# Respacing the first and the last transform of an interleaved SSM and FFN kernel

## The chip, the cores and the metric

The kernel runs on one core of one Trainium2 chip. The metric is the device time of one execution in microseconds (us), the median of three runs. Engines are called by their names or by those of the profile: TensorE (PE; PEld is its weight load), VectorE (DVE), ScalarE (ACT), GpSimd (POOL), and SyncE (SP), whose queue starts most DMA transfers.

## The reference

The reference computes the output and all gradients of a block that adds two branches to its input: an S4 layer (a long convolution whose filter comes from complex exponentials) and a gated feed-forward network with a ReLU gate. Cut to what matters:

```python
# x, grad_out: [1, 2048, 576] bf16; W_gate, W_up: [576, 4608]; W_down: [4608, 576]; A, B, C: [576, 128]
xn = layernorm(x)
# branch A: S4
dt = exp(log_dt)
P  = exp(dt * (A_re + 1j * A_im) [:, :, None] * arange(2048))
K  = einsum("dn,dnl,dn->dl", C, P, dt * B).real
y  = irfft(rfft(xn padded) * rfft(K padded))[:2048] + xn * Dskip
# branch B: gated feed-forward
gate = xn @ W_gate; gate = gate * (gate > 0)
h    = gate * (xn @ W_up)
out  = x + y + h @ W_down
# returned: out, and the gradients of x, A, B, C, log_dt, Dskip, W_gate, W_up, W_down for grad_out
```

## The kernel before

There are two sources of work. The feed-forward part (FFN) runs through 12 slices of the hidden dimension, c = 0 to 11, and is TensorE work nearly throughout. The S4 part is a Python generator that puts its instructions between those of the FFN. Each source yields its estimated us, and the driver lets the S4 part have the fraction `PACE` of the FFN's:

```python
PACE = 0.9
for us in ffn.gen(ln, final):
    if us == "last":                  # the final output needs the S4 part
        if s4_open: ...               # emit what is left of it
        continue
    ft += us
    ...
    while s4_open and stt < PACE * (ft - start):
        r = next(sgen, None)
        if r is None: s4_open = False
        else: stt += r
```

So a larger number yielded by the S4 part spreads the same instructions over more FFN work. A scheduler then sets the order in each engine's queue, near to this one.

The convolution is done by DFT in three stages per half of the 576 channels. `p1` transforms the input and the output gradient and brings the filter's gradient back; `p2` makes the filter and the parameter gradients; `p3` transforms the filter and brings back the results. Between the stages the data go through DRAM, because the next stage needs them in another layout. A pause (`yield gap`) gives the stores and the first loads time. `n` is the number of buffers: 4 where a transform stands alone in the kernel (the first, `p1(0)`, and the last, `p3(1)`), 2 or so where it runs beside `p2`.

```python
def both(self, a, wa, b, wb):         # interleaves two tasks in the ratio wa : wb
    ta = tb = 0.0
    for us in a:
        ta += us
        yield us
        while b is not None and tb * wa < ta * wb: ...   # next step of b, yielded too

def slow(self, f, task):
    for us in task: yield f * us

# in gen():
yield from self.both(self.p1(0, 4, 10.0), 68.0, self.params(pw), 45.0)
with ExitStack() as c:
    pools = self.p2_pools(c)
    yield from self.both(self.p2(0, pools, pw), 0.8 * W2, self.p1(1, 2, 3.0), W1)
    yield from self.both(self.p2(1, pools, pw), 0.8 * W2, self.p3(0, 2, 3.0), W3)
yield from self.p3(1, 4, 8.0)
```

The forward stage, line 628 in the profile, for ns signals (2 in `p1`, 1 in `p3`):

```python
def fwd1(self, hf, ns, load, ap, op, n, gap):
    ...
    for n2 in range(ST):              # ST = 16
        if n2 % 2 == 0:
            S1, sig = Sx.get(n2 // 2), sigs.get(n2 // 2)
            if n2 == 0: yield gap
        A = op.tile([P, 2, ns, DH], BF16, name=f"fA{ns}")          # DH = 288
        for ri in range(2):
            for i in range(ns):
                ps = self.ps()        # one of 3 PSUM buffers of the S4 part
                nc.tensor.matmul(ps[:, :DH], lhsT=S1[:, n2 % 2, ri, :], rhs=sig(i, n2), start=True, stop=True)
                g.bal.copy(A[:, ri, i, :], ps[:, :DH], DH)         # on VectorE or ScalarE
            if ri == 0: yield 0.2 * ns
        nc.sync.dma_start(self.A[ns][hf][:, n2], A[:])
        yield 0.2 * ns
```

The mixing stage (line 645, and 655 on the way back) and the back stage (line 686) of `p1`:

```python
    f = 1.0 if n < 4 else 1.25
    for h in range(ST + 1):
        if h < ST:
            b = bs.get(h)             # load of b_ug, n ahead
            if h == 0: yield gap
            for i in range(2):
                yield from self.slow(f, self.mix(sg[:, i], b[:, :, i, :]))
                yield f * 0.15
            ...                       # store of s_ug
            Z = self.product(fp, pp, sg[:, 1], sg[:, 0], True)
            yield f * 0.7
        if old is not None:
            yield from self.slow(f, self.unmix(Ct[:, :, 0, :], old))
            ...                       # store of C_dk
            yield f * 0.5
    # back stage: loads of bC1 in n + 1 buffers
    for n2 in range(ST):
        Ct = cs.get(n2)
        if n2 == 0: yield gap
        ...
        g.bal.copy(dk[:, :, n2 % 4, :], self.back2(S3[:, n2 % 2], Ct, 0)..., DH)
        yield 0.5
```

`p3` has a forward stage and a mixing stage (f = 2.0) alike. Its results (`C_ydu`, loaded as `bC2`) go into the output matmuls of the last FFN slice.

Beside `p1(0)` runs `params`. It loads the S4 parameters, makes their products, and in 36 steps the decay exponentials, each a multiplication on VectorE, an exponential on ScalarE and a store of 320 KB:

```python
def ex_step(i):
    v.tensor_tensor(ex[:], pw[:, 0, ...], self.ev[...], op=ALU.mult)      # line 585
    nc.scalar.activation(ex[:], ex[:], ACT.Exp)                            # line 586
    nc.sync.dma_start(self.ex_dram[:, i], ex[:])
    bal.add(d=0.75, a=0.65)
for i in range(0, 8):
    ex_step(i)
    yield 1.0
...                                   # products of the parameters, yields of 2 x 2.0
for i in range(8, D // SX):           # 8 to 35
    ex_step(i)
    yield 1.0
```

Of the kernel before, what the change touches and what calls it, by code (L numbers as in the profile page):

```python
# [20 lines left out]
L, D, F, N = 2048, 576, 4608, 128  # L21
# [10 lines left out]
SX = 16  # L32
# [61 lines left out]
def iota(nc, ap, pattern, base, mult):  # L94
    nc.gpsimd.iota(ap, pattern=pattern, base=base, channel_multiplier=mult, allow_small_or_imprecise_dtypes=True)
# [380 lines left out]
class S4:  # L476
# [85 lines left out]
    def params(self, pw):  # L562

        g, nc, bal = self.g, self.g.nc, self.g.bal
        v = nc.vector
        with ExitStack() as c:
            pool = self.pool(c, "par_raw", 1)
            exp_ = self.pool(c, "par_ex", 8)
            raw = pool.tile([P, 6, D], BF16, name="raw")
            nc.sync.dma_start(raw[:], self.par_in[:])  # L570
            ldt = pool.tile([P, D], BF16, name="ldt")
            nc.sync.dma_start(ldt[:], self.log_dt.rearrange("(o d) -> o d", o=1).to_broadcast([P, D]))
            yield 1.0
            dt = pool.tile([P, D], F32, name="dtf")
            nc.scalar.activation(dt[:], ldt[:], ACT.Exp)
            nc.sync.dma_start(self.dt_dram[:], dt[:])
            Ar, Ai, Br, Bi, Cr, Ci = (raw[:, i, :] for i in range(6))
            v.tensor_tensor(pw[:, 0, :], Ar, dt[:], op=ALU.mult)
            bal.add(d=0.7, a=0.7)
            yield 1.0  # L580

            def ex_step(i):
                shp = [P, SX, NE]
                ex = exp_.tile(shp, F32, name="exs")
                v.tensor_tensor(ex[:], pw[:, 0, i * SX:(i + 1) * SX].unsqueeze(2).to_broadcast(shp), self.ev[:].unsqueeze(1).to_broadcast(shp), op=ALU.mult)
                nc.scalar.activation(ex[:], ex[:], ACT.Exp)
                nc.sync.dma_start(self.ex_dram[:, i], ex[:])
                bal.add(d=0.75, a=0.65)

            for i in range(0, 8):  # L590
                ex_step(i)
                yield 1.0
            p1 = pool.tile([P, D], F32, name="p1")
            p2 = pool.tile([P, D], F32, name="p2")
            v.scalar_tensor_tensor(pw[:, 1, :], Ai, 1.0 / TWO_PI, dt[:], op0=ALU.mult, op1=ALU.mult)
            for j, (y1, y2, op) in enumerate(((Br, Bi, ALU.subtract), (Bi, Br, ALU.add))):
                v.tensor_tensor(p1[:], Cr, y1, op=ALU.mult)
                v.tensor_tensor(p2[:], Ci, y2, op=ALU.mult)
                v.tensor_tensor(p1[:], p1[:], p2[:], op=op)
                v.tensor_tensor(pw[:, 2 + j, :], p1[:], dt[:], op=ALU.mult)  # L600
                bal.add(d=2.6)
                yield 2.0
            for i in range(8, D // SX):
                ex_step(i)
                yield 1.0

# [82 lines left out]
    def p1(self, hf, n, gap):  # L689

        g, nc = self.g, self.g.nc
        cols = slice(hf * DH, (hf + 1) * DH)
        with ExitStack() as c:
            ap = self.pool(c, f"p1_a{hf}", n, "right")

            def load(m):
                t = ap.tile([P, 2, 2, DH], BF16, name="sig")
                nc.sync.dma_start(t[:, 0], g.xn_dram[:, 2 * m:2 * m + 2, cols])
                nc.sync.dma_start(t[:, 1], g.g_v[:, 2 * m:2 * m + 2, cols])
                return lambda i, n2: t[:, i, n2 % 2, :]  # L700
            yield from self.fwd1(hf, 2, load, ap, self.pool(c, f"p1_o{hf}", 2 * n - 2 * (n < 4), "right"), n, gap)
        with ExitStack() as c:
            bp = self.pool(c, f"p1_b{hf}", n, "right")
            fp = self.pool(c, f"p1_f{hf}", n, "right")
            pp = self.pool(c, f"p1_p{hf}", 1, "right")

            def load_b(h):
                b = bp.tile([P, 2, 2, DH], BF16, name="b_ug")
                nc.sync.dma_start(b[:], self.mix_in(self.A[2][hf], h))
                return b  # L710
            bs = Ahead(load_b, ST, n)
            Z = None
            f = 1.0 if n < 4 else 1.25
            for h in range(ST + 1):
                old, Z = Z, None
                if h < ST:
                    b = bs.get(h)
                    if h == 0:
                        yield gap
                    sg = fp.tile([P, 2, 2, DH], BF16, name="s_ug")  # L720
# [3 lines that stand above are left out]
                    nc.sync.dma_start(self.S[hf][h], sg[:])  # L724
# [3 lines that stand above are left out]
                    Ct = fp.tile([P, 2, 1, DH], BF16, name="fC1")  # L728
                    yield from self.slow(f, self.unmix(Ct[:, :, 0, :], old))
                    nc.sync.dma_start(self.mix_in(self.C[1][hf], h - 1), Ct[:])  # L730
                    yield f * 0.5
        with ExitStack() as c:
            bp = self.pool(c, f"p1_c{hf}", n + 1, "right")
            dp = self.pool(c, f"p1_d{hf}", 2, "right")

            def load_c(n2):
                Ct = bp.tile([P, 2, 1, DH], BF16, name="bC1")
                nc.sync.dma_start(Ct[:], self.C[1][hf][:, n2])
                return Ct
            Sx, cs = Ahead(self.dft(bp, self.s3_dram), ST // 2, n), Ahead(load_c, ST, n + 1)  # L740
            for n2 in range(ST):
                if n2 % 2 == 0:
                    S3 = Sx.get(n2 // 2)
                Ct = cs.get(n2)
                if n2 == 0:
                    yield gap
                if n2 % 4 == 0:
                    dk = dp.tile([P, DH // SC, 4, SC], BF16, name="dk")
                g.bal.copy(dk[:, :, n2 % 4, :], self.back2(S3[:, n2 % 2], Ct, 0).rearrange("p (g d) -> p g d", d=SC), DH)
                if n2 % 4 == 3:  # L750
                    nc.sync.dma_start(self.dk_dram[hf][:, n2 // 4], dk[:])
                yield 0.5

    def p3(self, hf, n, gap):

        g, nc, bal = self.g, self.g.nc, self.g.bal
        with ExitStack() as c:
            ap = self.pool(c, f"p3_a{hf}", n, "right")
            kp = self.pool(c, f"p3_k{hf}", 2, "right")
            kks = [None]  # L760

            def load(m):
                if m % 2 == 0:
                    kks[0] = kp.tile([P, DH // SC, 4, SC], BF16, name="kk")
                    nc.sync.dma_start(kks[0][:], self.k_dram[hf][:, m // 2])
                kk = kks[0]
                return lambda i, n2: kk[:, :, n2 % 4, :]
            yield from self.fwd1(hf, 1, load, ap, self.pool(c, f"p3_o{hf}", 2 * n - 2 * (n < 4), "right"), n, gap)
        with ExitStack() as c:
            bp = self.pool(c, f"p3_b{hf}", n, "right")  # L770
            fp = self.pool(c, f"p3_f{hf}", n, "right")
# [11 lines left out]
            f = 1.0 if n < 4 else 2.0  # L783
# [234 lines left out]
    def gen(self):  # L1018
        g, nc = self.g, self.g.nc
        self.make_dft16()  # L1020
        yield 1.0
        yield from self.make_dft128()
        with ExitStack() as cp:
            kp = self.pool(cp, "s4_par", 1)
            pw = kp.tile([P, 4, D], F32, name="pw")
            self.ev = kp.tile([P, NE], F32, name="ev")
            self.ones = kp.tile([P, 1], F32, name="ones")
            nc.vector.memset(self.ones[:], 1.0)
            iota(nc, self.ev[:, 0:16], [[1, 16]], 0, 0)
            iota(nc, self.ev[:, 16:24], [[256, 8]], 0, 0)  # L1030
            iota(nc, self.ev[:, 24:40], [[16, 16]], 0, 0)
            yield from self.both(self.p1(0, 4, 10.0), 68.0, self.params(pw), 45.0)
            with ExitStack() as c:
                pools = self.p2_pools(c)
                yield from self.both(self.p2(0, pools, pw), 0.8 * W2, self.p1(1, 2, 3.0), W1)
                yield from self.both(self.p2(1, pools, pw), 0.8 * W2, self.p3(0, 2, 3.0), W3)
            yield from self.p3(1, 4, 8.0)

class Final:

# [214 lines left out]
```

## Time and profile before

| | before |
|---|---|
| median of 3 runs | 1794.33 us |
| lowest, highest | 1794.07, 1795.59 us |
| span of the profiled execution | 1792.3 us |
| instructions in it | 42070 |
| DMA moved | 373.30 MB, mean 208 GB/s |
| share of packets' time on SyncE's queue (q1) | 52.4% of 16 engines |

The first transform runs from 95 to 285 us of the span, the parameter stage with the second and third transform beside it from about 300 to 1480 us, and the last transform from 1493 to 1619 us. A stretch of the span is read by the busy us of each engine in it, against its length.

### The profile page before, as it was taken

What the parts mean: (1) busy time and instruction counts of PE and PEld (TensorE: products, weight loads), DVE (VectorE), ACT (ScalarE), POOL (GpSimd) and SP (SyncE); (2) the same over time, 40 slices, a digit from 0 to 9 for tenths busy, and PEclk for the clock granted to TensorE, in tenths of its full rate; (3) what the DMA queues carried; (4) which work ended last, traced back from release to release, by engine and by line L of the source; (5) the groups of instructions that cost most, each with busy time, mean ns of one, the idle gap of its engine ahead of it and who ended that gap; (6) DMA issues with size and microseconds to landing.
All of it is one profiled execution on the core that took longest, in us unless ns stands there. A gap on an engine that the chain in (4) does not pass through costs nothing.

```text
span 1792.3 us, 42070 instructions
## 1 busy us (share of the span) xinstructions
PE 1719.7 (96%) x16449; PEld 1184.7 (66%) x16449; DVE 1317.8 (74%) x2867; ACT 1189.2 (66%) x2736; POOL 205.0 (11%) x246
## 2 busy tenths in 40 slices
PE   7989989999999999999999999999999998999998
PEld 5665557667667666766766766766676675676776
DVE  7575884677789788678787889889978962972551
ACT  5875874786688477568468658747857845864651
POOL 0200112011022011012101101101111100110000
PEclk9999999999999999999999999999999999999999
DMA  9799989679568656766858856866766578995873
GB/s 297 265 332 303 331 233 295 194 182 253 165 145 228 192 139 157 226 183 147 229 154 190 230 156 142 212 188 151 181 185 152 112 212 257 260 288 157 270 240 100
DMA packets 239004, 373.30 MB, mean 208 GB/s; under 512 B 49491, under 2 KB 153429, under 8 KB 237269
## 3 DMA queue, kind: packets, MB, share of 16 engines
q1 hardware_dynamic: 212836, 304.09, 52.4%
q0 software_dynamic: 24384, 51.92, 18.6%
q10 hardware_dynamic: 1584, 14.60, 2.3%
q8 instruction: 129, 2.11, 0.5%
q14 instruction: 71, 0.57, 0.1%
HBM read 233.10 MB, written 137.43 MB: 207 GB/s over the span
## 4 chain that ended last, share of the span: by engine, by line
PE 63%; DVE 21%; ACT 7%; DMA 6%; issue 3%; SPq 1%; POOL 0%; ACTq 0%; DVEq 0%; POOLq 0%
PE ps_mm L298 17%; PE ps_mm L244 15%; PE ps_mm L352 11%; PE ps_mm L336 6%; PE ps_mm L270 3%; DVE V L935 2%; DVE T L261 2%; DVE Sm L936 2%; DVE V L881 1%; DVE Y L882 1%; DVE Y L880 1%; DVE rg L254 1%; PE ps_mm L370 1%; DMA gT<-in_gT_dram 1%; DVE X L861 1%
## 5 line engine op out<-in xcount | busy, mean ns | idle before, releaser
L298 PE MATMUL ps_mm<-wf,T 128*128 128x288 bf16 x3456 | 481.8, 287 | 7.4 <-DVE T L256 2.6
L298 PEld LDWEIGHTS <-T 128*128 128x128 bf16 x3456 | 324.5, 98 | 97.0 <-issue 12.9
L68 ACT CAST osx<-ps_mm 128x288 bf16<-128x288 f32 x682 | 260.5, 428 | 50.5 <-PE ps_mm L298 47.6
L311 POOL DMA_DIRECT2D acc_dram<-osx x160 | 138.8, 867 | 1027.8 <-ACT osx L68 590.7
L352 PEld LDWEIGHTS <-rows 128*128 128x128 bf16 x1536 | 146.2, 98 | 95.4 <-issue 1.6
L244 PE MATMUL ps_mm<-xT,wd_150 128*128 128x512 bf16 x720 | 181.1, 379 | 4.1 <-ACT xT L153 1.6
L270 PEld LDWEIGHTS <-T 128*128 128x128 bf16 x1728 | 127.5, 98 | 86.3 <-issue 4.7
L244 PE MATMUL ps_mm<-xT,wd_151 128*128 128x512 bf16 x720 | 180.8, 380 | 0.0
L254 DVE SCALAR_TENSOR_TENSOR rg<-rg,ps_mm 128x512 bf16<-128x512 bf16 x144 | 98.2, 682 | 108.3 <-PE ps_mm L244 68.6
L244 PE MATMUL ps_mm<-gT,wd_152 128*128 128x512 bf16 x705 | 175.9, 379 | 0.7 <-DMA gT<-in_gT_dram 0.7
L270 PE MATMUL ps_mm<-ident_bf,T 128*128 128x128 bf16 x1728 | 157.6, 220 | 4.8 <-DVE T L256 1.9
L336 PE MATMUL ps_mm<-rows,hN 128*128 128x144 bf16 x2304 | 158.9, 227 | 0.0
L336 PEld LDWEIGHTS <-hN 128*128 128x128 bf16 x2304 | 148.5, 98 | 8.0 <-issue 5.4
L68 ACT CAST obw<-ps_mm 128x384 bf16<-128x384 f32 x103 | 49.2, 478 | 144.7 <-PE ps_mm L352 112.4
L352 PE MATMUL ps_mm<-dgN,rows 128*128 128x384 bf16 x768 | 136.8, 326 | 0.5 <-DMA rows<-xs_dram_141 0.5
L352 PE MATMUL ps_mm<-duN,rows 128*128 128x384 bf16 x768 | 135.6, 326 | 0.0
L253 ACT ACTIVATE rg<-ps_mm 128x512 bf16<-128x512 f32 x144 | 86.9, 603 | 52.1 <-PE ps_mm L244 51.5
L68 ACT CAST dhb<-ps_mm 128x512 bf16<-128x512 f32 x141 | 83.8, 594 | 49.6 <-PE ps_mm L244 47.7
L261 DVE TENSOR_TENSOR T<-dhb,rg 128x1024 bf16<-128x1024 bf16 x141 | 101.0, 717 | 19.4 <-ACT dhb L68 18.7
L244 PEld LDWEIGHTS <-wd_150 128*128 128x128 bf16 x720 | 66.0, 97 | 61.5 <-issue 3.7
L244 PEld LDWEIGHTS <-wd_151 128*128 128x128 bf16 x720 | 65.4, 98 | 59.9 <-issue 3.3
L244 PEld LDWEIGHTS <-wd_152 128*128 128x128 bf16 x705 | 63.4, 98 | 58.8 <-issue 1.8
(2506 smaller groups left out, 3042.2 us busy)
## 6 DMA issues: line engine op xcount, KB each, us to landing
acc_dram<-osx POOLq DMA_DIRECT2D x176, 288.0 KB, 5.1
gT<-in_gT_dram SPq DMA_DIRECT2D x48, 640.0 KB, 6.2
xT<-xT_dram SPq DMA_DIRECT2D x44, 640.0 KB, 5.8
rows<-in_gq_dram SPq DMA_DIRECT2D x48, 576.0 KB, 4.3
wf<-in_Wf_dram ACTq DMA_DIRECT2D x11, 1296.0 KB, 8.9
ex_dram<-exs SPq DMA_DIRECT2D x36, 320.0 KB, 4.6
ex<-ex_dram SPq DMA_DIRECT2D x36, 320.0 KB, 4.5
out_dram<-obw SPq DMA_DIRECT2D x96, 96.0 KB, 2.7
```

Source lines behind the costliest of these rows:

```text
L68: self.nc.scalar.copy(out, in_)
L244: nc.tensor.matmul(ps[:], lhsT=w[:, k, fs], rhs=rhs[:, k, :], start=(k == 0), stop=(k == NK - 1))
L253: nc.scalar.activation(rg, ps_g[:], ACT.Relu)
L254: nc.vector.scalar_tensor_tensor(upm, rg, 0.0, ps_u[:], op0=ALU.is_gt, op1=ALU.mult)
L261: nc.vector.tensor_tensor(T[:, 1:3], dhb.unsqueeze(1).to_broadcast([P, 2, JS * P]), ru[:], op=ALU.mult)
L270: nc.tensor.transpose(out=pt[:, j, :], in_=src[:, j * P:(j + 1) * P], identity=g.ident_bf[:])
L298: nc.tensor.matmul(ps[:, cs], lhsT=lt, rhs=rh, start=(i == 0), stop=(i == len(mms) - 1))
L311: nc.gpsimd.dma_start(g.acc_dram[:, t, :, :], o[:], accum_op=ALU.add)
L336: nc.tensor.matmul(ps[:, ft * 144:(ft + 1) * 144], lhsT=self.hN[:, st, ft * P:(ft + 1) * P], rhs=gq[:, st, :], start=(st == 0), stop=(st = ...
L352: nc.tensor.matmul(ps[:, :Fc], lhsT=xs[:, st, 0:P], rhs=src[:, st, :], start=(st == 0), stop=(st == ST - 1))
L935: nc.vector.tensor_tensor(pr[:, vi], X[:, dx:dx + DG, r0:r0 + 2].rearrange("p d r a -> p d (r a)").unsqueeze(2).to_broadcast(sh), psg[:, 0 ...
L936: nc.vector.tensor_reduce(out=Sm[:, :, s0 + dd:s0 + dd + DG, :].rearrange("p v d j -> p v (d j)"), in_=pr.rearrange("p v d j c -> p v (d j ...
```

## The change

It changes only yields and the place of one loop. The forward stage of the first transform is stretched 1.8 times and that of the last 2 times, pauses in them included; the back stage of the first transform yields 1 instead of 0.5. The mixing of the first transform is drawn together (1.1 for 1.25), and the pauses go from 10 and 8 to 6. The first eight exponential steps lose their place ahead of the parameter products, so all 36 come after these. The aim is to have fewer copies and transfers at a time in the two transforms that stand alone, so that TensorE needn't wait for them.

```diff
-            for i in range(0, 8):
-                ex_step(i)
-                yield 1.0
             p1 = pool.tile([P, D], F32, name="p1")
...
-            for i in range(8, D // SX):
+            for i in range(D // SX):
                 ex_step(i)
                 yield 1.0
... p1, forward stage:
-            yield from self.fwd1(hf, 2, load, ap, ..., n, gap)
+            yield from self.slow(1.0 if n < 4 else 1.8, self.fwd1(hf, 2, load, ap, ..., n, gap))
... p1, mixing:
-            f = 1.0 if n < 4 else 1.25
+            f = 1.0 if n < 4 else 1.1
... p1, back stage:
-                yield 0.5
+                yield 0.5 if n < 4 else 1
... p3, forward stage:
-            yield from self.fwd1(hf, 1, load, ap, ..., n, gap)
+            yield from self.slow(1.0 if n < 4 else 2, self.fwd1(hf, 1, load, ap, ..., n, gap))
... gen:
-            yield from self.both(self.p1(0, 4, 10.0), 68.0, self.params(pw), 45.0)
+            yield from self.both(self.p1(0, 4, 6), 79.04, self.params(pw), 45.0)
...
-            yield from self.p3(1, 4, 8.0)
+            yield from self.p3(1, 4, 6)
```

More of the change, by code (lines that the diff above doesn't have):

```diff
@@ L700, in load @@
                 return lambda i, n2: t[:, i, n2 % 2, :]
-            yield from self.fwd1(hf, 2, load, ap, self.pool(c, f"p1_o{hf}", 2 * n - 2 * (n < 4), "right"), n, gap)
+            yield from self.slow(1.0 if n < 4 else 1.8, self.fwd1(hf, 2, load, ap, self.pool(c, f"p1_o{hf}", 2 * n - 2 * (n < 4), "right"), n, gap))
         with ExitStack() as c:
@@ L767, in load @@
                 return lambda i, n2: kk[:, :, n2 % 4, :]
-            yield from self.fwd1(hf, 1, load, ap, self.pool(c, f"p3_o{hf}", 2 * n - 2 * (n < 4), "right"), n, gap)
+            yield from self.slow(1.0 if n < 4 else 2, self.fwd1(hf, 1, load, ap, self.pool(c, f"p3_o{hf}", 2 * n - 2 * (n < 4), "right"), n, gap))
         with ExitStack() as c:
```

## The prediction

> **What bounds the kernel now.** I read the page first: engines, then the slices, then the chain of waits; after that the same trace by stretches, and TensorE's waits in the stretches that the change touches.
>
> From the page of the kernel before (engine, busy us, share of the span, instructions; then tenths in 40 slices of 44.8 us):
>
> ```profile
> PE 1719.7 (96%) x16449; PEld 1184.7 (66%) x16449; DVE 1317.8 (74%) x2867; ACT 1189.2 (66%) x2736; POOL 205.0 (11%) x246
> PE   7989989999999999999999999999999998999998
> DMA  9799989679568656766858856866766578995873
> ```
>
> TensorE is the bound, and leaves 1792.3 - 1719.7 = 72.6 us in which it does nothing. Its 7 and 8 stand in slices 0, 2, 5, 33 and 39 (counted from 0), that is at the start, at 90 to 134, 224 to 269 and 1479 to 1523 us, and at the end; in the middle three the DMA row is at 9, 8 and 8. The rest is nearly full, so only these places can pay. Slice 0 is the load of the inputs and slice 39 the last weight gradients, which the change leaves alone.
>
> The stretches of the first transform (half 0 of the input side, the one that has no other half beside it) and of the last (half 1 of the output side), as busy us of each engine, then TensorE's clock, DMA share and GB/s:
>
> ```profile
> core 0: us, PE busy (x) PEld busy (x) DVE busy (x) ACT busy (x) POOL busy (x), PEclk, DMA share, GB/s
> 95.00:141.00 46.00, 38.48 (x342) 29.36 (x341) 33.37 (x62) 33.50 (x79) 2.88 (x6) 0.89 0.98 336
> 160.00:248.00 88.00, 83.50 (x634) 47.62 (x631) 71.04 (x188) 72.94 (x184) 6.81 (x8) 1.00 0.95 306
> 264.00:287.00 23.00, 17.27 (x141) 12.38 (x141) 16.57 (x39) 11.40 (x31) 2.63 (x3) 1.00 1.03 302
> 1493.00:1508.00 15.00, 13.14 (x100) 8.52 (x98) 2.84 (x6) 14.37 (x42) 0.11 (x1) 1.00 0.93 317
> 1508.00:1519.00 11.00, 6.86 (x49) 4.11 (x48) 3.60 (x8) 3.85 (x9) 1.61 (x2) 0.94 1.00 257
> 1529.00:1619.00 90.00, 88.93 (x763) 59.96 (x761) 74.16 (x229) 66.95 (x181) 10.35 (x12) 1.00 0.92 268
> ```
>
> 95 to 141 is the forward stage of the first transform, 160 to 248 its mixing, 264 to 287 its back stage; 1493 to 1508 is the forward stage of the last one, 1508 to 1519 the pause after it, 1529 to 1619 its mixing. TensorE loses 7.5, 4.5, 5.7, 1.9, 4.1 and 1.1 us in them. In 1493 to 1508 ScalarE is busy 14.37 of 15 us while VectorE does 2.84: the copies out of PSUM hold TensorE.
>
> What ended TensorE's idle time (the view of waits cut to these stretches: us in total, times, longest):
>
> ```profile
> PE ps_s_2099 L628 <- DVE fA_2069 L62: 3.1, 1, 3.1
> PE ps_s_1651 L628 <- ACT fA_1620 L68: 2.2, 1, 2.2
> PE ps_s_4104 L686 <- DMA bC_4060<-C_dk_183: 2.3, 1, 2.3
> PE ps_s_4273 L686 <- DMA bC_4223<-C_dk_183: 1.5, 1, 1.5
> PE ps_s_25366 L645 <- DMA b_k<-A_k_178: 4.1, 1, 4.1
> ```
>
> and three pieces of the chain of waits (start us, us, what):
>
> ```profile
> 125.72 7.75 DMA A_ug_179<-fA_1891
> 265.07 7.28 DMA bC_4060<-C_dk_183
> 277.60 6.14 DMA bC_4223<-C_dk_183
> ```
>
> So the forward stage waits for copies of `fA`; one of these copies waited 7.75 us for a store of the buffer before it. The back stage waits for loads of `bC1` that take 6 to 7 us. The first mixing of the last transform waits 4.1 us for its first load.
>
> **What the Trainium skill says.** "Perfetto Trace Analysis", section "Identifying the Most-Contended Engine": matmul busy time is no measure of how near the peak TensorE is. The trace agrees: the page has 379 ns for a 512-column matmul, while the chain has five in a row in 1.08 us, 216 ns each. "TensorE: Matmul & The Clock Gate", section "Wait — 56ns, not 53.3ns?", gives the same 215.7 ns. I therefore count work, 0.42 ns a column, and not busy time. The same page, section "What's actually happening", says that an idle window of about 3.4 us can halve the clock. The mean clock is 0.89 in 95 to 141 and 0.94 in 1508 to 1519 against 1.00 in most others, so a gap there costs a little more than its length. "DMA: Bandwidth & Descriptors", section "Issuing engines are not separate DMA queues": all queues share 16 engines. The trace agrees: at a DMA share near 1 the loads slow down for everybody, 7.28 us for a `bC1` load of 144 KB where loads of 128 to 144 KB have medians of 3 to 5 us over the run.
>
> **The change part by part.** Both programs hold the same 16447 matmuls; only their order differs. I walked through TensorE's own order in both and noted at how much finished feed-forward work (FFN, us at 0.42 ns a column) each stage of the transforms begins and ends:
>
> - first transform, forward: 22.4 us of FFN work before, 38.5 after; pause 18.9, then 11.8
> - mixing: 68.5, then 60.6; pause 9.3, then 7.3
> - back: 9.9, then 15.6
> - everything between (parameter stage, second and third transform) about 7 us later, at the same spacing
> - last transform, forward: 8.0, then 13.9; pause 5.7, then 6.9; mixing 79.7, then 78.5
> - from its last matmul to the first matmul of the final output: 29, then 13.
>
> Where nothing disturbs it, the kernel does about 0.96 us of counted work per us (the parameter stage, 301 to 1462 us of the span). Against this pace I take the excess of each stage.
>
> Forward, first transform. 64 matmuls of 288 columns are 64 x 0.12 = 7.7 us; with FFN 22.4 it is 30.1 us of work, 31.4 us at pace; it took 45.0 us (95.3 to 140.3): excess 13.6 us. Before, ten of the 64 stand in TensorE's order with no FFN matmul between them, just where the 2.2 us wait is, because three PSUM buffers serve them; after, that bunch is seven and the others two or three at a time. The same 64 copies of some 0.43 us and their exponentials (0.82 us on VectorE, 0.74 on ScalarE) now have 46.2/0.96 = 48 us of work to hide behind. But the move of the exponentials relieves little: ScalarE's order has 24 of the 36 before the first mixing copy now, and 28 after, since the stage is longer. The first eight only go behind the parameter products. And DMA stays at a share near 1. I give half: -6.5.
>
> Pause after it. Last forward matmul 140.3, first load of the mixing at 145.3, landing in about 5.8 us: 11 us are needed, 11.8/0.96 = 12.3 are there. +0.5 for the chance of a wait.
>
> Mixing. 7.9 us of FFN less to hide the same 192 copies and 16 products behind; VectorE has 71.0 of 88 us already. But 12 exponential steps in it become 8. +1.
>
> Pause before back. Last unmixing matmul 253.5, first back matmul 264.2: 10.7 us with a wait of 0.9. 7.3/0.96 = 7.6 us are there after. +2.
>
> Back. 9.9 + 32 x 0.12 = 13.8 us of work, 14.4 at pace, took 20.3: excess 5.9. Its 16 loads in five buffers at 7.2 us each need 11 x 7.2/5 = 16 us after the first five; 19.4/0.96 = 20 us are there after. -4.5.
>
> Last transform, forward. 8.0 + 3.8 = 11.8 us of work, 12.3 at pace, took 15.2: excess 2.9, copies on ScalarE alone. With 13.9 us of FFN: -2. Pause after it: the last store of `A_k` is issued at 1508.6, its load at 1513.4, the matmul comes at 1518.1; that chain stays, 1.2 us more work covers it: -1.
>
> The end. Last unmixing matmul 1618.8, first final matmul 1645.8, 27 us. Of these the store and load of the last spectra take about 7 us (issue of the store 1620.0, of the load 1622.7, 3.0 us to land). After, 13 of 29 is left, 27 x 13/29 = 12 us: still enough by 5. +0.7 for the chance that it isn't.
>
> Sum: -6.5 + 0.5 + 1 + 2 - 4.5 - 2 - 1 + 0.7 = -9.8 us. 1794.3 - 9.8 = 1784.5; I write **1785**.
>
> **The rivals.** (1) DMA is the real bound from 100 to 300 us. Its share is 0.95 to 1.03 in the three stages, and the bytes stay the same: the waits then move to other transfers (input loads, the mixing), and the first transform gives back only 2 or 3 us: about 1791. For it: two of the three waits are on loads or on a buffer held by a store. Against it: 240 to 260 us has a share well below 1 (0.83 in 248 to 264), so there is some room. (2) The shorter pauses become the wait: the store and load chains of 10 to 11 us stay and there is less to cover them, +3 to +5 in all, about 1789. The wait of 0.9 us already there speaks for it. (3) The last transform ends too late and the final output waits for its spectra: the 12 us of cover against 7 speak against it; with it, up to +5. (4) The excess of both forward stages goes altogether, -16 and -5 with the back stage: 1774.
>
> **Range and chances.** Below 1774 all the named excess would have to vanish; above 1796 two rivals would have to come together with a shift of the parameter stage against the FFN that costs a few us, which the reordering of every queue could do. So 1775 to 1796. 2% are 36 us, more than all the excess in the touched stages (13.6 + 5.9 + 2.9 and the wait of 4.1, 26.5 us): faster 0.02, within 0.96, slower 0.02.
>
> **What would show it.** In the profile after: the wait of `L628` for `fA` copies under 3 us in all and a clock above 0.95 in the forward stage (its share of the saving); waits on `bC1` loads mostly gone in the back stage but one of 2 to 3 us at its head (the pause); the wait for `b_k` near 3 us; ScalarE under 0.8 busy in the last forward stage; and no wait of the final matmuls on `bC2`. The prediction is wrong if the DMA share stays at 1 and TensorE's idle time between 95 and 300 us stays near 18 us, or if time is lost in the middle, from 300 to 1490 us, where the spacing is the same.

## The result: 1.2% slower, and the profile after

| | before | after |
|---|---|---|
| median, us | 1794.96 (4 runs) | 1818.69 (4 runs) |
| lowest, highest | 1794.07, 1796.92 | 1813.02, 1819.76 |
| span of the profiled execution | 1792.3 | 1817.8 |

The ratio is 1.0124, 95% interval 1.0101 to 1.0148: 24 us slower, where 10 us faster was predicted. The lines of the page after that answer to those shown of before (in the kernel after, line numbers above 590 are three lower, so 628, 645, 655 and 686 are now 625, 642, 652 and 683):

```profile
PE 1726.3 (95%) x16449; PEld 1188.6 (65%) x16449; DVE 1321.4 (73%) x2875; ACT 1186.7 (65%) x2728; POOL 203.7 (11%) x246
PE   7979987999999999999999999999999999999998
PEclk9989988999999999999999999999999999999999
DMA  8789979678667666866856856766675578895873
```

TensorE's idle time grew from 72.6 to 91.5 us. Its busy time grew too, by 6.6 us, for the same 16449 matmuls (the prediction counted 16447): the mean granted clock is 0.987, before it was 0.994. Slice 2 (91 to 136 us) fell from 8 to 7 and slice 6 (273 to 318 us) from 9 to 7; slice 5 is an 8 in both. The clock row, all 9 before, is at 8 in these three slices. The stretches after (columns as before: TensorE, weight loads, VectorE, ScalarE, GpSimd busy, then clock, DMA share, GB/s):

```profile
95.00:161.00 66.00, 54.50 (x460) 39.99 (x458) 42.19 (x73) 41.42 (x92) 3.21 (x7) 0.90 0.92 319
229.00:252.00 23.00, 16.39 (x102) 8.92 (x101) 12.14 (x32) 13.17 (x32) 1.69 (x2) 0.78 0.72 224
264.00:277.00 13.00, 8.36 (x64) 5.70 (x63) 10.09 (x20) 5.49 (x13) 1.69 (x2) 0.97 0.89 218
298.00:305.00 7.00, 0.93 (x8) 0.71 (x7) 0.18 (x1) 0.00 (x0) 0.00 (x0) 0.64 1.04 351
```

The forward stage (95 to 161) still leaves 11.5 us of TensorE idle. Then there are three holes: late in the mixing (229 to 252) 6.6 us, at the head of the back stage (264 to 277) 4.6 us, and near its end (298 to 305) 6.1 of 7 us. In the first and the last of these every engine is idle for long, so no engine is the bound there. The waits of TensorE and of VectorE in the forward stage and in these holes (us in total, times, longest):

```profile
PE ps_s_1939 L625 <- DVE fA_1905 L62: 5.7, 1, 5.7
PE ps_s_3633 L642 <- DVE s_ug L62: 4.6, 1, 4.6
PE ps_s_3645 L642 <- DVE s_ug L62: 2.0, 1, 2.0
PE ps_s_4032 L683 <- DMA bC_3933<-C_dk_183: 4.6, 1, 4.6
PE ps_s_4349 L683 <- DMA wf<-in_Wf_dram: 6.1, 1, 6.1
DVE xa L841 <- DMA ex_dram<-exs: 9.4, 1, 9.4
```

**Where the time went.** TensorE's order is known for both programs. I took the time at which each had done the same FFN work, and took off what it had done more or less of the transforms' work by then (at 0.96 us of work per us). The result is the us by which a kernel lags behind the one before at that point. The columns are us of FFN work: 106 is the end of the forward stage after, 170 falls late in the mixing, 186 is the first back matmul after, 206 is past its end, 206 to 1180 is the parameter stage, and 1440 is close to the end. Each row rests on one profiled execution of a kernel.

| lag, us | 106 | 160 | 170 | 186 | 196 | 206 | 700 | 900 | 1180 | 1440 |
|---|---|---|---|---|---|---|---|---|---|---|
| after | 3.7 | 3.8 | 11.0 | 14.5 | 9.9 | 17.1 | 15.1 | 21.2 | 24.3 | 25.1 |
| a_exp_early | 3.8 | 3.3 | 1.0 | 1.9 | -2.1 | 5.2 | 3.9 | 7.8 | 11.4 | 11.1 |
| a_mem | 3.7 | 4.5 | 2.2 | 5.9 | 1.7 | 10.6 | 8.4 | 13.7 | 16.9 | 18.4 |
| a_mem_pause | 3.1 | 3.1 | 0.8 | -1.5 | -4.8 | 3.8 | 5.6 | 10.2 | 13.4 | 13.4 |
| a_unshift | 3.3 | 2.7 | 7.3 | 10.5 | 7.2 | 14.2 | 10.3 | 10.9 | 14.0 | 13.0 |
| a_repair | 2.8 | 2.4 | 0.1 | -2.2 | -1.4 | -2.2 | 1.7 | 1.8 | 5.6 | 3.3 |
| b_exp_late | 6.9 | 6.1 | 8.5 | 8.2 | 9.4 | 8.4 | 9.1 | 9.5 | 9.3 | 7.7 |
| b_shift | -1.1 | -0.8 | -0.8 | -0.8 | 0.3 | -0.7 | 1.8 | 9.7 | 10.3 | 7.8 |
| b_fwd_only | 2.2 | 0.3 | -1.9 | -4.2 | -8.7 | 3.8 | 6.5 | 8.7 | 9.9 | 9.6 |
| b_mem_back | 0.3 | 0.8 | -1.6 | -2.6 | -7.7 | 2.4 | 0.2 | 0.4 | 0.5 | -0.5 |
| best1 | 1.8 | 1.4 | -1.0 | 5.2 | -0.2 | -1.8 | 0.8 | 1.5 | 1.6 | -0.2 |

The kernel after lags 3.7 us by the end of the forward stage, gets 7.2 more between 160 and 170, some 3.5 to the head of the back stage and 7.2 at its end (196 to 206), with 4.6 made up between these two, and 9 between 700 and 1180. The last transform adds about 1. The rows below it belong to the experiments.

### The profile page after: what moved, and what is told of

Same layout as the page of the kernel before. It is cut to its first block, busy times and chain, and to the rows that moved or that the text cites. A ratio compares the mean times of both kernels' runs of the same rounds, so it can differ in the third digit from the quotient of the medians.

```text
span 1817.8 us, 42080 instructions
## 1 busy us (share of the span) xinstructions
PE 1726.3 (95%) x16449; PEld 1188.6 (65%) x16449; DVE 1321.4 (73%) x2875; ACT 1186.7 (65%) x2728; POOL 203.7 (11%) x246
```

## The experiments

Names that begin with a_ are edits of the kernel after, those with b_ of the kernel before. Ratios are to the kernel before, run beside each on the same chip.

| run | median us | ratio, 95% interval |
|---|---|---|
| a_mem | 1813.20 | 1.0108, 1.0090 to 1.0126 |
| a_exp_early | 1806.35 | 1.0075, 1.0056 to 1.0094 |
| b_exp_late | 1800.35 | 1.0038, 1.0024 to 1.0051 |
| b_shift | 1802.07 | 1.0048, 1.0033 to 1.0063 |
| b_pause | 1794.73 | 1.0012, 1.0000 to 1.0024 |
| a_mem_pause | 1806.11 | 1.0062, 1.0044 to 1.0079 |
| b_shift_minus | 1812.45 | 1.0100, 1.0078 to 1.0123 |
| a_last_only | 1792.32 | 0.9990, 0.9982 to 0.9998 |
| b_fwd_only | 1803.82 | 1.0039, 1.0026 to 1.0052 |
| b_mem_back | 1794.23 | 0.9998, 0.9986 to 1.0010 |
| a_repair | 1802.00 | 1.0037, 1.0024 to 1.0049 |
| best1 | 1795.48 | 1.0001, 0.9991 to 1.0012 |
| a_unshift | 1807.35 | 1.0072, 1.0059 to 1.0086 |

(a_last_only, in spite of its letter, is the kernel before with the last part of the change.)

### The hole late in the mixing: a multiplication waits for a store, and the copies wait behind it

VectorE in the kernel after, in order of time (start us, us, what, and in brackets its idle time before and what ended that):

```profile
232.60 0.64 DVE L668 TENSOR_TENSOR pr_z<-pr_t,pr_w 64x288 bf16<-64x288 bf16 x2
242.60 0.82 DVE L841 TENSOR_TENSOR xa<-pw,ev 128x640 f32<-128x640 f32 x1 [9.36 <-DMA ex_dram<-exs]
243.35 0.45 DVE L62 CAST s_ug<-ps_s_3563 128x288 bf16<-128x288 f32 x1
```

The first multiplication of the parameter stage (`xa`) stands in VectorE's queue among the mixing copies, and waits for the store of an exponential. The copy of `s_ug` behind it can run only then, and TensorE has no PSUM buffer left. The stores and when SyncE issued them (the tile `exs` in the kernels before and after: count, shortest, median and longest ns of the issue, first and last start in us):

```profile
L587 SPq DMA_DIRECT2D ex_dram<-exs x36: 319/475/1320, 102.3 to 206.3; - x36
```

```profile
L586 ACT ACTIVATE exs<-exs x36: 725/740/825, 103.0 to 206.4; 128x640 f32<-128x640 f32 x36
L587 SPq DMA_DIRECT2D ex_dram<-exs x36: 319/445/1517, 103.9 to 234.4; - x36
```

The first of these two views is of the kernel before: its last store is issued at 206.3. After, the last exponential is computed at much the same time (206.4), but its store is issued at 234.4. SyncE's queue has stores and loads of the mixing and of the FFN ahead of it.

**a_mem.** A tile of the parameter stage waits for an exponential's store only if it takes over its memory. So its pool was put behind the others:

```diff
-  ... ("k_ex", 2), ("k_x", 1), ("k_xo", 2), ("k_uv", 1), ("k_yo", 4), ("k_yt", 2)
+  ... ("k_ex", 2), ("k_xo", 2), ("k_uv", 1), ("k_yo", 4), ("k_yt", 2), ("k_x", 1)
```

> The changed kernel with the parameter stage's pools in another order, so that the tile xa of its first multiplication lies in memory that the exponentials' tiles never used. TensorE's order stays the same but for a few rows. Theory (the late exponentials hold the parameter stage's first multiplication, which stands in VectorE's queue ahead of the mixing copies, by memory that it takes over): the wait of 9.36 us for the stores of the exponentials goes, and 6 to 8 us of the 24 with it, about 1811 us. Rival (the mixing is simply too dense for VectorE and ScalarE): the wait moves to the copies, about 1818 us.

Measured 1813.2 us, 3 us (by ratios) to 5 us (by medians) faster than the kernel after, less than the 6 to 8 expected. The interval of the ratio overlaps that of the kernel after, so the total alone proves little. But the trace shows the 9.4 us wait gone, and the lag at 170 is 2.2 us for 11.0; 6.5 us of that are left at 206. The memory that it takes over is what held the multiplication.

**a_exp_early.** The loop over the first eight exponentials goes back to its place.

```diff
+            for i in range(0, 8):
+                ex_step(i)
+                yield 1.0
...
-            for i in range(D // SX):
+            for i in range(8, D // SX):
```

> The changed kernel with the first eight exponential steps back ahead of the parameter products, nothing else. Theory (the exponentials are too late): their last store lands some 5 us earlier, the 9.36 us wait gets shorter and the 5.7 us wait of the forward stage, where a copy stands behind a multiplication that waits for a store, changes place: 5 to 10 us faster than the changed kernel, 1809 to 1814 us. Rival (the pauses and the mixing are at fault): within 2 us of 1818.

Measured 1806.35 us, 9 us (by ratios) to 12 us (by medians) faster than the kernel after, at the top of what was expected or above it. The hole late in the mixing is gone too (1.0 us at 170): the multiplication runs at 231.8 without a wait. Either repair removes the hole, so it needed both the shared memory and the late exponentials. The wait at the head of the back stage is shorter (1.9 us for 4.6), the one at its end stays (6.9 us). The forward stage did not gain by it (3.8 for 3.7).

**b_exp_late.** The same loop moved in the kernel before, as in the change's first two hunks.

> The kernel before with all exponential steps after the parameter products, nothing else. Theory: the last exponential comes later and eight more multiplications wait for stores in VectorE's queue: 3 to 8 us slower than 1795. Rival: no change, within 1 us.

Measured 1800.35 us, 6 to 7 us slower. Here 6.9 us are lost in the forward stage, where TensorE waits 7.3 us at one go for a copy of `fA`, while a multiplication in VectorE's queue waits 7.1 us for a store. This move costs time alone and in the change, though not in the same place.

### The forward stage: stretching it doesn't free the copies

The kernel after, VectorE in the forward stage:

```profile
129.37 0.82 DVE L585 TENSOR_TENSOR exs<-pw,ev 128x640 f32<-128x640 f32 x1 [5.51 <-DMA ex_dram<-exs]
130.12 0.45 DVE L62 CAST fA_1905<-ps_s_1931 128x288 bf16<-128x288 f32 x1
```

The copy at 130.12 is not late because VectorE is full: VectorE stood still for 5.51 us, since the multiplication ahead of the copy waited for one of the eight `exs` buffers, which a store held. It is the same pattern as above. And it was there before the change, in the wait of 3.1 us for `fA_2069` that the prediction shows. The kernel before, VectorE and then ScalarE:

```profile
133.24 0.82 DVE L585 TENSOR_TENSOR exs<-pw,ev 128x640 f32<-128x640 f32 x1 [5.89 <-DMA ex_dram<-exs]
134.50 0.45 DVE L62 CAST fA_2069<-ps_s_2070 128x288 bf16<-128x288 f32 x1
```

```profile
131.47 0.47 ACT L68 CAST fA_2069<-ps_s_2073 128x288 bf16<-128x288 f32 x1
```

ScalarE wrote into `fA_2069` at 131.47, so that buffer was free by then. The copy at 134.50 stood behind the multiplication, which waited for a store of an exponential.

**b_fwd_only.** Only the forward stage is stretched; a negative yield puts the parameter stage back to its place.

```diff
-            yield from self.fwd1(hf, 2, load, ap, ..., n, gap)
+            yield from self.slow(1.0 if n < 4 else 1.8, self.fwd1(hf, 2, load, ap, ..., n, gap if n < 4 else gap / 1.8))
-            yield from self.both(self.p1(0, 4, 10.0), 68.0, self.params(pw), 45.0)
+            yield from self.both(self.p1(0, 4, 10.0), 79.04, self.params(pw), 45.0)
+            yield -10.2
```

> The kernel before with only the forward stage of the first transform stretched 1.8 times (its pause left at 10, the exponentials in their old order but spread with it), and the parameter stage begun where it was. The prediction gave this stretch -6.5 us. If copies and their density hold TensorE there: 4 to 8 us faster than 1794.5. If the copies wait because a multiplication for an exponential stands ahead of them in VectorE's queue and waits for an earlier exponential's store: within 3 us of 1794.5, with a wait of over 5 us for a copy of fA.

Measured 1803.82 us, 7 to 8 us slower; the expectation of the theory was missed as well. The stage itself lags 2.2 us, with a wait of 6.3 us for a copy of `fA`, which stood behind a multiplication that waited 7.07 us for a store; so stretching it brought nothing. The rest is lost elsewhere: its back stage now lies at 198 to 207 us of FFN work, and between 196 and 206 the lag jumps by 12.5 us:

```profile
PE ps_s L686 <- DMA bC<-C_dk: 12.5, 5, 8.0
PE ps_s L628 <- DVE fA L62: 9.5, 2, 6.3
```

### The back stage: it runs into the next slice's loads

**b_mem_back.** Only the back stage is stretched, with the memory of a_mem, the parameter stage in its old place.

```diff
-                yield 0.5
+                yield 0.5 if n < 4 else 1
...
+            yield -8.0          # after the first transform
```

> The kernel before with the back stage of the first transform stretched (1 for 0.5), the parameter stage's first multiplication in memory of its own, and the parameter stage begun where it was. Theory (the stretched back stage reaches into the stretch where the next slice's inputs and weights are loaded, and its last bC1 loads stand behind them): a wait of 4 us or more on bC1 near its end, 2 to 7 us slower than 1794.5. Rival, as the prediction had it (a stretched stage gives its loads time): 3 to 5 us faster.

Measured 1794.23 us, no difference: neither the slower nor the faster total came. Both mechanisms are in the trace. Up to 196 the stage runs 5 us better than before, as predicted (-2.6 to -7.7). Then one wait gives it all back. TensorE, and then SyncE and ScalarE just ahead of it in the same kernel:

```profile
287.53 0.64 PE L686 MATMUL ps_s<-bC,Sx 128*128 128x288 bf16 x2 [8.39 <-DMA bC<-C_dk]
```

```profile
272.70 0.38 SPq L202 DMA_DIRECT2D xT<-xT_dram  x1
274.25 2.11 SPq L738 DMA_DIRECT2D bC<-C_dk  x3
276.41 0.50 SPq L196 DMA_DIRECT2D gT<-in_gT_dram  x1
```

```profile
276.75 0.34 ACTq L191 DMA_DIRECT2D wf<-in_Wf_dram  x1
```

Loads of `bC1` issued from 274.3 us on are waited for until 287.5, in the company of 640 KB each of `xT` and `gT` and 1296 KB of `wf`; the median of all such loads in that run is 3.7 us. In the kernel after it is the same: the load of `bC_4265` is issued at 291.0, `gT` at 292.3, `wf` at 294.4, and its matmul runs at 304.2, while DMA moves 351 GB/s (the row 298 to 305 above). The wait is put down to `wf` there, but the matmul reads `bC1`. Before, the stage ended at 196, ahead of these loads: its last `bC1` load is issued at 279.2, `xT` at 281.4, `wf` at 286.8 and `gT` at 293.2.

**b_pause.** The three pauses cut to 6, with 12 us given back afterwards.

```diff
-            yield from self.both(self.p1(0, 4, 10.0), 68.0, self.params(pw), 45.0)
+            yield from self.both(self.p1(0, 4, 6), 68.0, self.params(pw), 45.0)
+            yield 12.0
```

> The kernel before with the three pauses of the first transform cut from 10 to 6, and 12 us given back after it, so that the later stages end up where they were. Theory (the pauses cover chains of 10 to 11 us of store, load and landing, and their cut becomes a wait): TensorE waits 3 to 5 us for the first bC1 load of the back stage and 0 to 2 us at the first mixing; 3 to 6 us slower than 1794.5. Rival (the waits of the back stage come from crowded DMA alone): within 2 us.

Measured 1794.73 us, ratio 1.0012: some 2 us, and by the interval at most 4, where 3 to 6 were expected. The wait at the head of the back stage did come (3.4 us), but by the end of the stage it had been made up (lag 6.1 at 186, 1.0 at 190 and at 206).

**a_mem_pause.** a_mem, with the pause ahead of the back stage alone at 10 again.

```diff
                 if n2 == 0:
-                    yield gap
+                    yield 10.0 if n == 4 else gap
...
+            yield -4.0          # after the first transform
```

> The changed kernel with the parameter stage's first multiplication in memory of its own (as in a_mem), and the pause ahead of the back stage back at 10; the parameter stage begins where it does in the changed kernel. Theory (the short pause costs the 5 us at the head of the back stage): 3 to 6 us faster than a_mem's 1813. Rival (the back stage waits because input and weight loads of the FFN share the DMA engines at that place): within 2 us of 1813, with a wait of 5 us or more on bC1 elsewhere in the stage.

Measured 1806.11 us, 7 us faster than a_mem (8 by ratios); the lag at 186 goes from 5.9 to -1.5. So in the kernel after the short pause does cost what it hardly costs in the one before. The wait at the end of the stage stays (5.1 us for `bC1`, a lag of -4.8 that becomes 3.8): both halves of the expectation hold, each for its own wait.

### The middle: the parameter stage stands elsewhere

**b_shift** and **b_shift_minus** only move the parameter stage and what follows, by 7 us of FFN work later or earlier.

```diff
             yield from self.both(self.p1(0, 4, 10.0), 68.0, self.params(pw), 45.0)
+            yield 6.4           # b_shift_minus: -6.4
```

> The kernel before with a pause of 6.4 us between the first transform and the parameter stage, which puts the parameter stage, the second and third transform 7 to 8 us of FFN work later, where the changed kernel has them; the first transform stays. Theory (the 8 us that the changed kernel loses between 700 and 1330 us come from another fit of the parameter stage to the FFN): 5 to 8 us slower than 1795. Rival (they follow from the first transform or from which engine the copies fall to): within 2 us of 1795.

> The kernel before with the parameter stage and what follows 7 us of FFN work earlier (a pause of minus 6.4 us). It tells whether the 7.7 us of b_shift are a price of any displacement or of this one. If the place before was a tuned optimum: 3 to 8 us slower than 1794.5. If the fit is a matter of which FFN work a group of parameter steps meets: anywhere between 5 us faster and 8 us slower, with the difference again between 700 and 900 us.

Measured 1802.07 and 1812.45 us: 8 and 18 us slower. The place before was the best of the three. The 18 us lie beyond both ranges expected for b_shift_minus, and not where they were expected: by the measure of the table its lag is about 0 at 206, 11 at 700 and 18 at 1180. The reason stays open. b_shift loses nothing in the first transform and 8 us between 700 and 900, as the kernel after does (15.1 to 21.2). What makes it there is not shown. From 925 to 1115 us VectorE's waits for ScalarE's sines grow from 7.5 to 12.6 us (four each), while those for the sums' matmuls (`V`) shrink from 9.8 us to 7.9. The longest waits for sines in the kernel before, then all of b_shift:

```profile
DVE A_15709 L854 <- ACT W L849: 4.1, 1, 4.1
DVE A_16332 L854 <- ACT W L849: 1.8, 1, 1.8
```

```profile
DVE A L854 <- ACT W L849: 12.6, 4, 4.2
```

**a_unshift** undoes the displacement in the kernel after.

```diff
             yield from self.both(self.p1(0, 4, 6), 79.04, self.params(pw), 45.0)
+            yield -6.6
```

> The changed kernel with a pause of minus 6.6 us after the first transform, so that the parameter stage and what follows stand at the FFN work where they stood before; the first transform keeps all of the change. Theory (the displacement costs the same 7 us here as in b_shift): 1809 to 1813 us, with the difference to the kernel before constant between 700 and 1330 us. Rival (the loss in the middle is a consequence of the copies' other distribution): within 3 us of 1818.

Measured 1807.35 us, 9 us (by ratios) to 11 us (by medians) faster than the kernel after, at the top of what was expected or above it. From 700 to 900 its lag is constant (10.3 to 10.9) where the kernel after loses 6 us, so that loss is the displacement's; 3 us more up to 1180 come in both. It also lost 3 us less in the first transform: the multiplication late in the mixing waits 7.1 us for 9.4.

### The last transform

**a_last_only.** The kernel before with the change of `p3(1)` alone (stretch of 2, pause of 6).

> The kernel before with the change to the last transform alone (its forward stage stretched twofold, its pause 6). In the changed kernel this transform gave back 4 us in its pause and lost them to two waits of 3.2 us on the loads of kk. Theory (the two balance): within 2 us of 1794.5. Rival (the two waits on kk came from the displacement that the stages before had given it): 2 to 5 us faster than 1794.5.

Measured 1792.32 us, ratio 0.9990, interval 0.9982 to 0.9998: a gain of 2 us, the only one in the study and barely clear of the noise; its trace agrees (a lag of 0 at 1180 and -1.7 at 1440). In the kernel after, the 4.1 us wait for `b_k` is gone, but TensorE waits twice for the loads of `kk`:

```profile
PE ps_s_25313 L625 <- DMA kk<-k_dram_190: 3.2, 1, 3.2
PE ps_s_25381 L625 <- DMA kk<-k_dram_190: 3.2, 1, 3.2
```

Alone these two don't come, and a wait of 2.1 us for `b_k` stays. Both the lost and the new waits go with the displacement: b_shift, with the old last transform, waits 4.0 us for `kk` and not for `b_k`; a_unshift, with the new one, waits 4.3 us for `b_k` and 0.7 us for `kk`. What holds the loads of `kk` was not tried.

### Together

**a_repair** has the repairs of a_exp_early, a_mem and a_mem_pause, the back stage at 0.5 and the parameter stage in its old place (`yield -2.4`).

> The changed kernel with four repairs together: the first eight exponentials early, the parameter stage's first multiplication in memory of its own, the back stage as before with its pause of 10, and the parameter stage begun where it was before. What stays of the change is the stretched forward stage, the denser mixing, two shorter pauses and the whole of the last transform. If the named causes (the late exponentials with the memory, the back stage and its pause, the displacement) are all of it: 1790 to 1797 us. If some of the 24 us has another cause: 1800 us or more.

Measured 1802.0 us. Of the 24 us some 17 are gone, but not all, though in the profiled execution, which spans 1795.5 us, the lag is only 3.3. Its runs lie between 1797.3 and 1804.7, so what remains is partly not in the trace at hand. Some of the 24 us thus has another cause than those named, and it stays open.

**best1** has what looked harmless or good: pauses of 6, a back stage stretched but ending at 190, the memory of a_mem, the last transform as changed, and the parameter stage in its place (`yield 4.0`).

> The kernel before with what the runs showed to be harmless or good: the three pauses of the first transform at 6, so that its back stage begins earlier; the back stage stretched (1 for 0.5), now ending at 190 us of FFN work, ahead of the next slice's loads; the parameter stage begun where it was, with its first multiplication in memory of its own; and the changed last transform. Theory (the stretched back stage pays 4 to 5 us where it does not meet these loads, the last transform 2): 1786 to 1791 us. Rival (its loads wait wherever it stands): 1793 to 1798 us.

Measured 1795.48 us, no difference, as its rival had it. The back stage no longer meets the slice's loads (the lag at 206 is -1.8). But with the short pause it begins with a wait of 4.5 us for its first load (a lag of 5.2 at 186), so that what it gains up to 196 mostly makes this up. Then the FFN's weight gradients wait for a load, which they don't in the kernel before. The wait, SyncE in best1, and SyncE before:

```profile
PE ps_mm L352 <- DMA rows<-xs_dram: 3.2, 1, 3.2
```

```profile
299.39 0.52 SPq L824 DMA_DIRECT2D dkr<-dk_dram  x1
300.00 1.04 SPq L323 DMA_DIRECT2D rows<-xs_dram  x2
```

```profile
293.87 0.48 SPq L323 DMA_DIRECT2D rows<-xs_dram_141  x1
```

The load of `rows` stands behind a load of `dkr`, and so is issued at 300.0 instead of 293.9. SyncE issued nothing for 9 us before that load. From 286 to 310 us the DMA share is 0.72 to 0.78: this is again a queue held up, rather than transfers at their limit. It isn't the price of the stretched back stage either, since b_shift, with the old one, waits 2.7 us at the same place.

## Why the prediction was wrong, by its own steps

By the lags of the kernel after, the terms that were to sum to -9.8 us came out at 3.7 (forward), 5.6 (the pause after it and the mixing, up to 180), 5.2 (pause before back, 180 to 186), 2.6 (back), 7.2 (206 to 1180) and 0.8 (last transform), 25.1 together. The forward stage is off by 10 us, the middle and the back stage by 7 each.

- **The bound, and that only the gaps between 95 and 300 us and near 1500 us can pay:** the gaps were read rightly, but a place that has nothing to give can still lose. The middle was booked at zero ("about 7 us later, at the same spacing"). The displacement costs 6 to 8 us there (a_unshift, b_shift).
- **Forward stage, -6.5:** it became +3.7. The step that failed is "64 copies [...] now have 46.2/0.96 = 48 us of work to hide behind". The copies did not lack time; they stood in line behind multiplications that waited for stores (5.51 us at one go). The trace of before was misread here: "one of these copies waited 7.75 us for a store of the buffer before it", where the copy of `fA_2069` stood behind a multiplication that waited 5.89 us for a store of an exponential. The prediction saw that the exponentials were not relieved, and still gave half.
- **Pause after it, +0.5:** right in the kernel after, which shows no wait for `b_ug` of half a microsecond or more.
- **Mixing, +1:** about +5.5 (3.8 at 160 to 9.3 at 180). The count of exponentials was right, and density was not the matter: without the hole, a_mem lags 4.5 us at 160 and 2.2 at 170. One multiplication of the next stage, hoisted into the mixing, waited 9.36 us for a store in memory that it took over. The prediction had looked at TensorE's and ScalarE's order, and not at SyncE's, in which the last store moved back.
- **Pause before back, +2:** right in kind. The wait was 4.6 us for the first loads; the lag rose by 5.2 from 180 to 186.
- **Back stage, -4.5:** the mechanism is real (-5 up to 196 in b_mem_back) and was taken back by a wait of 6 to 8 us on the last loads, which the prediction took at 7.2 us each. At the stretched stage's end they took 13 us, beside 2.6 MB of the FFN's loads.
- **Last transform, -3:** -2 alone. In the kernel after it gave about +1, with the two waits on `kk` that go with the displacement.
- **The end, +0.7:** right: the final matmuls begin 10.8 us after the last unmixing, the prediction said 12, and they wait for nothing.
- **The rivals:** (1), DMA as the bound of this part, and (2), the pauses as the wait, were both at work. Each was priced at a smaller gain, though, and neither as a loss. Above 1796, the prediction said, two rivals would have to come together with a shift of the parameter stage that costs a few us. All three came, and the forward stage and the mixing lost time besides. Of its signs of being wrong, time was lost in the middle, and TensorE's idle time in the first transform did not stay but rose (19.7 us from 95 to 310 before, 31.4 from 95 to 330 after). Here a reordering of every queue lost more than the stages it was made for had to give.

## What to carry to other kernels

In these traces work that was ready stood behind an instruction that waited, on VectorE (9.36 us) and in SyncE's queue. Before moving work, look in every queue, also in that of the DMA issues, for what an instruction that waits will hold up behind it, and for buffers or memory that it takes over from a transfer. Stretching a stage is not free when what follows moves with it: check which loads of the other work its end will now meet, and keep the place of the later stages. A stage can give its gain back at its next load, as b_mem_back did with its 5 us when its end met the next slice's loads.

## What was not expected of the hardware

With about 2.6 MB of other loads issued around it, a load of 144 KB took 13.0 us from issue to landing in the kernel after (the one issued at 291.0), and up to 13.5 us in b_mem_back, where the median of such loads is 3.7 us. The clock was lower around the waits of TensorE: 0.64 in 298 to 305 us with the wait of 6.1 us, and 0.78 in 229 to 252 with 4.6 and 2.0. So matmuls after a hole ran slower too: the two on `bC_4265`, right after the 6.1 us, took 399 and 447 ns, those on `bC_4245` before it 286 and 297 ns.
